# The keys' maximum one projection group later, and the first weights on ScalarE's DMA queue, in a fused attention and Fourier-filter kernel

## The chip, the core and the metric

The kernel runs on one core of one Trainium2 chip. The metric is the device time of one execution in microseconds (us); lower is better. The core has TensorE (PE, matrix products), VectorE (DVE), ScalarE (ACT), GpSimd (POOL) and SyncE (SP), each with its own instruction queue that it works through in order, and 16 DMA engines that SP, ACT and POOL give transfers to.

## The reference

Two independent results are computed from two inputs of 2048 tokens by 448 channels and put side by side.

```python
q = (x @ wq).reshape(B, S, H, Dh)          # H = 16 heads, Dh = 28
k, v = x @ wk, x @ wv                      # one key and one value head for all 16
p = softmax(q k^T * Dh**-0.5)
a = concat_heads(p @ v) @ wo               # first half of the output
X = rfft2(x_b, axes=(tokens, channels)) * (w_r + 1j * w_i)
b = irfft2(X)                              # second half of the output
```

## The kernel before

The kernel has two stages. The **first stage**, up to about 70 us, projects the tokens to queries, keys and values and does the first half of the Fourier transform. The **second stage**, the remaining 560 us, is attention with the rest of the transform woven in; its order of work on TensorE, VectorE and ScalarE is written out by hand (`PLAN`). The change touches only the first stage, which ends where the first score product (L918) starts.

Single precision is carried by splitting every operand into a rounded high part and a remainder: `split_x` and `split_w` copy a raw tile to the high part and subtract to get the low part, and `proj` multiplies high by high, high by low and low by high. Tokens are worked in four chunks `c` of 512, projected outputs in four groups `g` of 128, channels in four parts `j`. Chunk 0 and the first part of chunk 1 are done part by part while their data arrive; after that the loop `for c ... for g` does one group at a time: eight or eleven projection products, `evac(c, g)` (ScalarE copies the result to `qraw`, VectorE reduces it to the largest absolute value, `qmx`), and behind some groups a unit of the transform.

A unit `q` of the transform (there are eight) has a load, a fold, a first product `fft1_a` (64 small matmuls, L155) and a second product `fft1_b` (16 matmuls, L174). The fold runs on VectorE: two operations on the halves (L130), a sum and a difference (L132, L133), which `fft1_fold(q, 0)` issues, and four more (L136 to L139), which `fft1_fold(q, 1)` issues; without a part it issues all eight.

The softmax is shifted by a bound instead of a true maximum. For this the largest absolute key is needed once: `qm` (L459, VectorE) reduces `qmx` of the first two groups over all chunks, `key_max` (L377 to L380) brings it into place with two matmuls (four passes) on TensorE and copies it to `kmb` on VectorE, `terms` (L286, VectorE) multiplies `kmb` with the queries' maxima, and `shift` (L291, L292) sums on TensorE and copies to `cvec` on VectorE. It is done for chunk 0 first, so that `build_q(0, 0)` (L232, L234, L223) can make the first query tile, and for the other chunks at the end (`terms(1, NC)`, `shift(1, NC)`, then `cmax`, L483, which the small products L487 check against a limit). The keys are also collected: `fetch` moves rows of `qraw` to `kf`, on SP or on POOL's DMA queue, and 16 transposes (L498) turn the values.

The order on TensorE in the first stage is the order of the program. The order on the other engines is made by a scheduler from dependences and priorities; `behind(a, b)` adds that `a` is issued after `b` on its engine, without a wait between engines. Raw tiles (256 KB each) come from a pool named `raw` with eight buffers, the weights' first tile in three pieces, and all of these transfers are issued by SP.

Of the kernel before, what the change touches and what calls it, by code (L numbers as in the profile page):

```python
# [10 lines left out]
F32 = mybir.dt.float32  # L11
# [4 lines left out]
ALU = mybir.AluOpType  # L16
# [49 lines left out]


WARM = 10, 6


@with_exitstack
def kernel(ctx: ExitStack, tc: tile.TileContext, t: dict):
    nc = tc.nc
# [49 lines left out]
    def fft1_fold(q, part=None):  # L123
        x = xb[q][0][:113]
        e2, o2 = x[:, 0:2], x[:, 2:4]
        if part != 1:
            f = ff[q] = fp.tile([113, 4, 4, 2, 32], F32, name="f", tag="wi")
            xv = x.rearrange("p k (j h m) -> p k j h m", h=2, m=32)
            for h, op in enumerate((ALU.add, ALU.subtract)):
                nc.vector.tensor_tensor(f[:, :, :, h], xv[:, :, :, 0], xv[:, :, :, 1], op=op)  # L130
            y = f.rearrange("p k j h m -> p k (j h m)")
            nc.vector.tensor_tensor(e2, y[:, 0::2], y[:, 1::2], op=ALU.add)  # L132
            nc.vector.tensor_tensor(o2, y[:, 0::2], y[:, 1::2], op=ALU.subtract)  # L133
        if part != 0:
            y = ff[q].rearrange("p k j h m -> p k (j h m)")
            return [nc.vector.tensor_tensor(y[:, 0], e2[:, 0], e2[:, 1], op=ALU.add),  # L136
                    nc.vector.tensor_tensor(y[:, 1], e2[:, 0], e2[:, 1], op=ALU.subtract),
                    nc.vector.tensor_tensor(y[:, 2], o2[:, 0], o2[:, 1], op=ALU.subtract),
                    nc.vector.tensor_tensor(y[:, 3], o2[:, 0], o2[:, 1], op=ALU.add)]  # L139

    at1, stored = {}, []

    def fft1_a(q):
        for p in range(2):
# [112 lines left out]
    with tc.tile_pool(name="w1", bufs=1) as w1:  # L257
# [27 lines left out]
        def terms(c0, c1):  # L285
            return nc.vector.tensor_scalar(prod[:, :, c0:c1], qmx[:, :, c0:c1], kmb, None, op0=ALU.mult)  # L286
# [6 lines left out]

        halves = slice(0, 1024), slice(1024, 2048)
        with tc.tile_pool(name="x1", bufs=2) as x1:
            warm = x1.tile([1, 1], F32, name="warm")
            nc.vector.memset(warm, 0.0)
            nc.scalar.activation(warm, warm, AF.Exp)
# [9 lines left out]
                zeros(n)  # L308

            def raw(src, eng):  # L310
                r = x1.tile([128, 512], F32, name="raw", bufs=8)
                eng.dma_start(r, src)
                return r


            first = slice(0, 128), slice(128, 256), slice(256, 512)
            xr, wr = {}, {}
            xr[0, 0] = raw(t["xa"][0, :, 0], nc.sync)
            wr[0] = x1.tile([128, 512], F32, name="raw", bufs=8)
            for s in first:  # L320
                nc.sync.dma_start(wr[0][:, s], t["wq"][:, 0, s])

            xr[1, 0] = raw(t["xa"][1, :, 0], nc.sync)
            for j in range(1, NK):
                xr[0, j] = raw(t["xa"][0, :, j], nc.sync)
                wr[j] = x1.tile([128, 512], F32, name="raw", bufs=8)
                for s in (slice(0, 256), slice(256, 512)):
                    nc.sync.dma_start(wr[j][:, s], t["wq"][:, j, s])

# [23 lines left out]
            def proj(pq, xh, xl, g, j, some=(0, 1, 2)):  # L353

                gs = slice(g * 128, (g + 1) * 128)
                parts = ((wqh, xh), (wqh, xl), (wql, xh)) if j < 3 else ((wqh, xh), (wql, xh))
                for n, (w, x) in enumerate(parts):
                    if n in some:
                        mm(pq, w[:, j, gs], x[:, j], start=(j == 0 and n == 0), stop=(j == 3 and n == 1))

            def evac(c, g, pq):
                cs = slice(c * CW, (c + 1) * CW)
                out = nc.scalar.activation(qraw[:, g, cs], pq, AF.Copy)
                nc.vector.tensor_reduce(qmx[:, g, c:c + 1], qraw[:, g, cs], axis=AX.X, op=ALU.max,
                                        apply_absolute_value=True)
                return out
# [8 lines left out]
            def key_max():  # L375

                pb = bank()  # L377
                for k in range(2):
                    mm(pb[:, 0:1], sel[:, k], qm[:, k:k + 1], start=(k == 0), stop=(k == 1))
                nc.vector.tensor_copy(kmb, pb[:, 0:1])  # L380
# [42 lines left out]
            for c in range(1, NC):  # L423
                for g in range(NG):
                    pq = pq1[g] if c == 1 else bank()
                    for j in range(1 if c == 1 else 0, NK):
                        proj(pq, *xs[c], g, j)
                    last = evac(c, g, pq)
                    if g == 0 and c < 3:
                        parts_of(c + 1)  # L430
                        for j in range(NK):
                            split_x(*xs[c + 1], c + 1, j)
                            if c < 2:
                                xr[c + 2, j] = raw(t["xa"][c + 2, :, j], nc.sync)
                    if c == 1 and g == 1:
                        fetch(range(7), halves[0])
                    if c == 3 and g == 1:
                        fetch(range(7), halves[1])
                    if c == 2 and g == 3:
                        fetch(range(7, 14), slice(0, 1536), nc.gpsimd)  # L440
                    if c == 3 and g == 2:
                        fetch(range(7, 12), slice(1536, S), nc.gpsimd)
                    if c == 1 and g == 0:
                        fft1_fold(1)
                    if c == 2 and g == 3:
                        keys(0)
                    n = 4 * (c - 1) + g
                    if n in slots:
                        q = slots.index(n)
                        fft1_a(q)  # L450
                        fft1_load(q + 4)
                        if n == 10:

                            terms(0, 1)
                            shift(0, 1)
                            qf, qh, ql = build_q(0, 0, True)
                        if n == 9:

                            top = nc.vector.tensor_reduce(qm, qmx[:, 0:2], axis=AX.X, op=ALU.max)  # L459
                            for ins in fft1_fold(5, 1):  # L460
                                behind(ins, top)
                        if q < 6:
                            fft1_fold(q + 2, None if q not in (3, 5) else 0)
                        if q:
                            fft1_b(q - 1)
                        if n == 9:
                            key_max()
            fetch(range(12, 14), slice(1536, S), nc.gpsimd)


# [5 lines left out]
            copy_q(i, 3, qf, ql, nc.gpsimd)  # L476
        behind(copy_q(1, 1, qf, ql, nc.scalar), last)
        top = terms(1, NC)
        for ins in fft1_fold(7, 1):
            behind(ins, top)  # L480
        last = fft1_b(5)
# [26 lines left out]
    d, f, a, b, e, c = free  # L508
# [450 lines left out]
    c = NC - 1  # L959
# [227 lines left out]
```

## Time and profile before

| what | us |
|---|---|
| median of three runs | 635.23 (634.75 to 635.24) |
| the profiled execution's own time | 635.08 |
| its span in the profile | 633.3 |
| busy in the span: PE | 627.4 (99%) |
| busy: DVE | 439.9 (69%) |
| busy: ACT | 546.9 (86%) |
| granted TensorE clock | 1.0 throughout |

All times in the profile are microseconds from the span's start; a row of the timeline gives start, duration, engine, line, operation and tiles, and in brackets the engine's idle time before it with what ended it. PE is the matmul row, PEld the loading of weights beside it. Matmuls overlap, so what one costs is read from start to start.

### The profile page before, as it was taken

The page shows a single profiled execution, that of the slowest core. Times are in us where ns is not written, and L with a number is a line of the kernel's source. Part 1 is how long each engine was busy: PE and PEld are TensorE (multiplying, and loading weights), DVE is VectorE, ACT ScalarE, POOL GpSimd, SP SyncE. Part 2 cuts the span into 40 slices and gives each one's busy share as a digit, 9 for nine tenths or more (in the row PEclk, how much of TensorE's full clock was granted, in tenths as well). Part 3 has the DMA queues.
Part 4 walks back from the last instruction along what each step waited for, and adds up shares of the span by engine and source line. Part 5 has one row for each costly group of instructions (what it writes and reads, how often), then busy time and mean ns, then how long its engine had stood idle before and what let it go on. Part 6 is the DMA issues. An engine that isn't in the chain of part 4 may idle for free. (4 is left out here: it accounts for less than half of the span.)

```text
span 633.3 us, 12165 instructions
## 1 busy us (share of the span) xinstructions
PE 627.4 (99%) x4437; PEld 377.7 (60%) x4437; DVE 439.9 (69%) x793; ACT 546.9 (86%) x984; POOL 61.5 (10%) x118
## 2 busy tenths in 40 slices
PE   9999999999999999999999999999999999999997
PEld 7877645646565655646565665565566565555555
DVE  5999648789998943866766845277687764457653
ACT  5554999999999998988989989998989989989991
POOL 4021501011113110000110100001010100000000
PEclk9999999999999999999999999999999999999999
DMA  8865863456455522216340513034152413030011
GB/s 254 288 177 168 261 167 87 115 146 177 124 152 124 139 65 66 76 64 187 77 106 18 125 37 82 16 83 147 35 129 60 98 55 91 16 82 11 21 31 61
DMA packets 37891, 66.74 MB, mean 105 GB/s; under 512 B 8009, under 2 KB 22746, under 8 KB 36860
## 3 DMA queue, kind: packets, MB, share of 16 engines
q1 hardware_dynamic: 32608, 52.50, 30.2%
q0 software_dynamic: 4640, 12.48, 7.7%
q8 instruction: 36, 0.59, 0.4%
q10 hardware_dynamic: 576, 0.92, 0.4%
q14 instruction: 31, 0.25, 0.1%
HBM read 29.81 MB, written 17.87 MB: 75 GB/s over the span
## 5 line engine op out<-in xcount | busy, mean ns | idle before, releaser
L853 ACT ACTIVATE p<-s 128x512 f32<-128x512 f32 x405 | 222.1, 638 | 27.3 <-PE s L918 26.5
L918 PE MATMUL s<-qa,ka 128*128 128x512 f32 x756 | 227.6, 402 | 0.0
L918 PEld LDWEIGHTS s<-qa,ka 128*128 128x128 f32 x756 | 138.1, 188 | 60.9 <-issue 26.8
L924 DVE COPY k<-s 128x512 f32<-128x512 f32 x122 | 80.1, 684 | 62.9 <-PE s L918 62.7
L864 PE MATMUL s<-p,vs 128*32 128x512 f32 x976 | 121.3, 595 | 0.0
L853 ACT ACTIVATE qraw<-s 128x512 f32<-128x512 f32 x137 | 79.2, 655 | 6.5 <-PE s L918 6.5
L943 ACT ACTIVATE k<-k 128x1024 f32<-128x1024 f32 x80 | 83.5, 1145 | 0.0
L864 PEld LDWEIGHTS s<-p,vs 128*32 128x32 f32 x976 | 29.4, 109 | 64.3 <-issue 59.4
L918 PE MATMUL sx<-qa,ka 128*128 128x512 f32 x137 | 55.3, 403 | 0.0
L918 PE MATMUL po<-qa,ka 128*128 128x512 f32 x131 | 53.2, 406 | 0.0
L853 ACT ACTIVATE p<-po 128x512 f32<-128x512 f32 x75 | 48.2, 642 | 4.5 <-PE po L918 4.2
L864 PE MATMUL s<-qraw,vs 128*32 128x512 f32 x384 | 49.5, 593 | 0.0
L853 ACT ACTIVATE p<-sx 128x512 f32<-128x512 f32 x64 | 41.5, 649 | 3.0 <-PE sx L918 2.9
L738 POOL DMA_DIRECT2D ol<-ol x36 | 18.0, 508 | 229.0 <-DVE ol L761 156.9
L864 PE MATMUL s<-k,vs 128*32 128x512 f32 x304 | 39.7, 594 | 0.0
L918 PEld LDWEIGHTS sx<-qa,ka 128*128 128x128 f32 x137 | 25.7, 188 | 11.1 <-issue 4.2
L918 PEld LDWEIGHTS po<-qa,ka 128*128 128x128 f32 x131 | 24.6, 188 | 11.3 <-issue 5.0
L868 DVE STREAM_TRANSPOSE osb<-s 128x512 f32<-128x512 f32 x13 | 9.3, 716 | 28.0 <-PE s L864 27.9
L864 PEld LDWEIGHTS s<-qraw,vs 128*32 128x32 f32 x384 | 12.0, 110 | 27.3 <-issue 26.1
L924 DVE COPY k<-po 128x512 f32<-128x512 f32 x17 | 11.6, 685 | 21.4 <-PE po L918 21.3
L853 ACT ACTIVATE qraw<-sx 128x512 f32<-128x512 f32 x35 | 22.9, 653 | 2.0 <-PE sx L918 2.0
L924 DVE COPY p<-s 128x512 f32<-128x512 f32 x35 | 23.0, 681 | 0.0
(277 smaller groups left out, 973.5 us busy)
## 6 DMA issues: line engine op xcount, KB each, us to landing
qa<-qa SPq DMA_DIRECT2D x15, 512.0 KB
raw<-xa SPq DMA_DIRECT2D x16, 256.0 KB
xb<-xb SPq DMA_DIRECT2D x8, 512.0 KB
qa<-qh SPq DMA_DIRECT2D x64, 64.0 KB
qa<-ql SPq DMA_DIRECT2D x60, 64.0 KB
t<-bs SPq DMA_DIRECT2D x16, 225.0 KB
wr<-wr POOLq DMA_DIRECT2D x16, 225.0 KB, 3.8
wi<-wi POOLq DMA_DIRECT2D x16, 225.0 KB, 5.2
```

Of the source, the lines that this page charges most:

```text
L738: nc.gpsimd.dma_start(ol[c][o, g].bitcast(F32), ol[c][r, 0].bitcast(F32))
L853: nc.scalar.activation(tiles[-1][:, h % 2], sc, AF.Exp, scale=SCALE)
L864: mm(po[c, g][32 * i:32 * i + 32], vs[:, kc], ps[i // 2][:, i % 2], start=(n == 1), stop=(n == 16))
L868: nc.vector.transpose(o, po[c, g])
L918: begun.append(mm(sc, ka[:, kc * 128:(kc + 1) * 128], qa[c, g][:, h], start=True, stop=True))
L924: nc.vector.tensor_copy(keep[i][h // 2][:, h % 2], sc)
L943: nc.scalar.activation(p, p, AF.Exp, scale=SCALE)
```

## The change

Two edits go together.

- The keys' maximum: `key_max()` moves from the end of the transform's unit behind group (3, 1) to directly behind the projection products of group (3, 2), ahead of that group's evacuation. The fold of unit 6 is cut in two parts like those of 5 and 7, and its last four operations are issued behind `terms(0, 1)`. For units 6 and 7 the last operation of the first part (L133 before) is issued behind `terms(0, 1)` and `terms(1, NC)`.
- The start: the three pieces of the first weights' tile are issued by ScalarE, ahead of its first activation, instead of by SP between the first two token tiles. The pool `raw` has twelve buffers instead of eight.

```diff
+RAW = 12
...
-            nc.vector.tensor_tensor(o2, y[:, 0::2], y[:, 1::2], op=ALU.subtract)
+            fold_end[q] = nc.vector.tensor_tensor(o2, y[:, 0::2], y[:, 1::2], op=ALU.subtract)
...
+            first = slice(0, 128), slice(128, 256), slice(256, 512)
+            xr, wr = {}, {}
+            wr[0] = x1.tile([128, 512], F32, name="raw", bufs=RAW)
+            for s in first:
+                nc.scalar.dma_start(wr[0][:, s], t["wq"][:, 0, s])
             warm = x1.tile([1, 1], F32, name="warm")
             nc.vector.memset(warm, 0.0)
             nc.scalar.activation(warm, warm, AF.Exp)
...
             xr[0, 0] = raw(t["xa"][0, :, 0], nc.sync)
-            wr[0] = x1.tile([128, 512], F32, name="raw", bufs=8)
-            for s in first:
-                nc.sync.dma_start(wr[0][:, s], t["wq"][:, 0, s])
 
             xr[1, 0] = raw(t["xa"][1, :, 0], nc.sync)
...
                     for j in range(1 if c == 1 else 0, NK):
                         proj(pq, *xs[c], g, j)
+                    if (c, g) == (3, 2):
+                        key_max()
                     last = evac(c, g, pq)
...
-                            terms(0, 1)
+                            top = terms(0, 1)
+                            behind(fold_end[6], top)
+                            for ins in fft1_fold(6, 1):
+                                behind(ins, top)
                             shift(0, 1)
...
-                            fft1_fold(q + 2, None if q not in (3, 5) else 0)
+                            fft1_fold(q + 2, None if q < 3 else 0)
                         if q:
                             fft1_b(q - 1)
-                        if n == 9:
-                            key_max()
...
         top = terms(1, NC)
+        behind(fold_end[7], top)
         for ins in fft1_fold(7, 1):
             behind(ins, top)
```

More of the change, by code (lines that the diff above doesn't have):

```diff
@@ L310, in raw @@
             def raw(src, eng):
-                r = x1.tile([128, 512], F32, name="raw", bufs=8)
+                r = x1.tile([128, 512], F32, name="raw", bufs=RAW)
                 eng.dma_start(r, src)
                 return r
-            first = slice(0, 128), slice(128, 256), slice(256, 512)
-            xr, wr = {}, {}
             xr[0, 0] = raw(t["xa"][0, :, 0], nc.sync)
-            wr[0] = x1.tile([128, 512], F32, name="raw", bufs=8)
-            for s in first:
-                nc.sync.dma_start(wr[0][:, s], t["wq"][:, 0, s])
             xr[1, 0] = raw(t["xa"][1, :, 0], nc.sync)
@@ L325 @@
                 xr[0, j] = raw(t["xa"][0, :, j], nc.sync)
-                wr[j] = x1.tile([128, 512], F32, name="raw", bufs=8)
+                wr[j] = x1.tile([128, 512], F32, name="raw", bufs=RAW)
                 for s in (slice(0, 256), slice(256, 512)):
```

2 lines of the change are left out of this document (1 added, 1 removed).

## The prediction

> **What bounds the kernel now.** I read the page's engine parts first, then the stretches of ten microseconds of the first stage, then the timeline of each engine around the places that the change touches, and last what waits for the keys' collected rows.
>
> ```profile
> PE 627.4 (99%) x4437; PEld 377.7 (60%) x4437; DVE 439.9 (69%) x793; ACT 546.9 (86%) x984; POOL 61.5 (10%) x118
> 40.00:50.00 10.00, 10.00 (x115) 7.88 (x112) 9.96 (x20) 5.18 (x9) 1.38 (x3) 1.00 0.59 164
> 50.00:60.00 10.00, 9.27 (x180) 6.97 (x178) 9.93 (x25) 4.36 (x8) 2.33 (x5) 1.00 0.65 185
> 60.00:70.00 10.00, 10.00 (x203) 7.89 (x200) 9.23 (x23) 7.18 (x13) 5.54 (x11) 1.00 0.76 206
> PE s L379 <- DVE qm L459: 0.7, 1, 0.7
> ```
>
> The columns of the stretches are PE, PEld, DVE, ACT and POOL busy, granted clock, DMA share, GB/s. TensorE is busy 99% of the span, so the time is the sum of its matmuls and its few gaps. In the first 72 us its own list of waits has, apart from the wait for the very first instruction, one entry: the 0.7 us of the keys' maximum, which is the 9.27 of 50 to 60. VectorE is busy 9.96 and 9.93 of 10 there: it is the second bound, a few tenths behind. In attention TensorE's gaps come to nothing that the list shows, so whatever shifts the first score product at 69.64 shifts the end by as much. A change of the first stage is therefore worth what it takes from TensorE's chain up to 69.64, and no more than VectorE and the transfers let through.
>
> **The change part by part. The old place of the maximum.** TensorE's timeline, a normal hand-over from the transform to a projection group first, then the one with the maximum, then the hand-over where the maximum will stand:
>
> ```profile
> 39.73 0.36 PE L174 MATMUL po<-a,fw 64*64 64x225 f32 x2
> 40.01 0.50 PE L359 MATMUL s<-xh,wqh 128*128 128x512 f32 x1
> 52.91 0.36 PE L174 MATMUL po<-a,fw 64*64 64x225 f32 x2
> 53.99 0.61 PE L379 MATMUL s<-qm,sel 128*128 128x1 f32 x4 [0.73 <-DVE qm L459]
> 54.46 0.49 PE L359 MATMUL s<-xh,wqh 128*128 128x512 f32 x1
> 56.87 0.39 PE L359 MATMUL s<-xh,wql 128*128 128x512 f32 x1
> 57.19 1.76 PE L155 MATMUL s<-cs,f 113*32 113x113 f32 x64
> ```
>
> From start to start the normal hand-over is 40.01 - 39.73 = 0.28 us, the one with the maximum 54.46 - 52.91 = 1.55. Taking it out saves 1.27 us.
>
> **The new place.** The four passes do not vanish; they now stand between the last projection product of group (3, 2) and the transform's 64. What such an insertion costs is shown by `shift`, two passes between the transform's products, against the same stretch without it:
>
> ```profile
> 32.06 1.76 PE L155 MATMUL s<-cs,f 113*32 113x113 f32 x64
> 33.74 0.41 PE L174 MATMUL pbb<-a,fw 64*64 64x225 f32 x2
> 58.88 0.39 PE L291 MATMUL s<-prod,blk 128*128 128x4 f32 x2
> 59.19 0.41 PE L174 MATMUL pbb<-a,fw 64*64 64x225 f32 x2
> ```
>
> Without: 33.74 - 32.06 = 1.68. With: 59.19 - 57.19 = 2.00. So two passes cost 0.32, which is the lower end; the upper end is the 0.61 that the four passes were busy. I take 0.45, near the 0.47 from 53.99 to 54.46. Net of this part: -1.27 + 0.45 = **-0.82 us**, between -0.95 and -0.66, if the maximum finds its input ready and nobody waits for its output. Both are read from VectorE:
>
> ```profile
> 53.06 0.68 DVE L364 TENSOR_REDUCE qmx<-qraw 128x1 f32<-128x512 f32 x1
> 53.78 0.16 DVE L459 TENSOR_REDUCE qm<-qmx 128x2 f32<-128x8 f32 x1
> 55.20 1.28 DVE L130 TENSOR_TENSOR f<-xb 113x512 f32<-113x512 f32 x2
> 56.40 0.15 DVE L380 COPY kmb<-s 128x1 f32<-128x1 f32 x1
> 57.73 0.22 DVE L286 TENSOR_SCALAR prod<-qmx,kmb 128x4 f32<-128x4 f32 x1
> 63.06 0.68 DVE L133 TENSOR_TENSOR xb<-f 113x512 f32<-113x512 f32 x1
> 64.38 0.23 DVE L286 TENSOR_SCALAR prod<-qmx,kmb 128x12 f32<-128x12 f32 x1
> ```
>
> `qm` is ready at 53.94. In the changed kernel TensorE comes to the maximum at about 56.87 - 1.27 + 0.3 = 55.9, so that wait is gone with two microseconds to spare. The copy to `kmb` can then run at about 56.4, where VectorE already has it now. `terms(0, 1)` follows; what waits for it is `shift(0, 1)` on TensorE, at 58.88 - 0.82 = 58.1. Before, it ended at 57.95, 0.15 ahead of that; the new ties put it ahead of the last fold operation L133, 0.6 us earlier, so it has cover of 0.75. The four later operations of unit 6 stay behind it as they are now, and their reader `fft1_a(6)` is 4 us away. I cost the ties of unit 6 at nothing. The tie of unit 7 does the same for `terms(1, NC)`: it took place at 64.38, behind L133 at 63.06, and TensorE will ask for it at 65.44 - 0.82 = 64.6 (row below); moved ahead of L133 it is ready by about 64.0. Without the tie it would be a stall of up to 0.1.
>
> **The start.** Issues and first consumers, and two of the stretches of one microsecond (columns as above):
>
> ```profile
> 0.76 0.41 SPq L312 DMA_DIRECT2D raw<-xa  x1
> 1.23 1.36 SPq L321 DMA_DIRECT2D raw<-wq  x3
> 3.95 0.43 DVE L345 CAST xh<-raw 128x512 fp32r<-128x512 f32 x1 [2.90 <-DMA raw<-xa]
> 4.15 0.51 ACT L339 ACTIVATE wqh<-raw 128x128 fp32r<-128x128 f32 x2 [1.89 <-DMA raw<-wq]
> 4.52 0.72 PE L359 MATMUL s<-xh,wqh 128*128 128x512 f32 x1
> 2.00:3.00 1.00, 1.00 (x6) 0.70 (x5) 0.00 (x0) 0.24 (x2) 0.94 (x2) 1.00 0.92 272
> 3.00:4.00 1.00, 1.00 (x6) 0.75 (x5) 0.05 (x1) 0.00 (x0) 1.00 (x3) 1.00 0.79 200
> 17.43 1.29 DVE L130 TENSOR_TENSOR f<-xb 113x512 f32<-113x512 f32 x2 [0.98 <-DMA xb<-xb]
> ```
>
> The first product starts 0.14 us after the first token tile is cast (3.95 + 0.43 = 4.38) and about as long after the first weights' piece is copied (half of 0.51 behind 4.15, 4.40). Both have to come earlier for the start to move, and the token tile was already issued first, at 0.76. The change issues the weights' pieces at the same moment from another queue. So the weights may come up to 0.47 us earlier (1.23 - 0.76), which alone is worth nothing, and the token tile may come later by what is mixed into it: one piece is 64 KB, at the 272 GB/s of the stretch 2 to 3 that is 0.24 us; all 256 KB would be 0.96. The other end is a gain: the first weights' piece took 4.15 - 1.23 = 2.92 from issue to use and the token tile 3.19; if the tile came as quickly, 0.27. I take **+0.1 us**, between the gain and one piece, nearer to the piece, because all that is certain is that the two now share the engines from the first byte.
>
> The Trainium skill (DMA: Bandwidth & Descriptors, "Issuing engines are not separate DMA queues") says that transfers started by ScalarE and SP run on the same 16 DMA engines and interleave, and that starting them from several engines saves only the issuing time. It speaks against this edit for the first token tile and leaves the queue behind it its issuing time; by it alone the start would be 0.24 later instead of 0.1, and the sum 0.14 less of a gain. No row of the kernel before has two such queues at work at once.
>
> What the edit does give is SP's time: 1.36 us of issuing lie between the first and the second token tile, and the DMA engines had room meanwhile (200 GB/s where they had moved 272, a share of 0.79). The next tiles come earlier by 72 KB at 272 GB/s, 0.26 us, up to 1.36. TensorE does not wait for them (its list has no such wait). VectorE does: it sat idle for 0.98 us before 17.43, waiting for the first unit's tile, and is full from there on. So VectorE's whole chain can start earlier by 0 to 0.98; I take **0.3**. ScalarE's three issues, at some 0.45 each, hold its first activation back until about 2.1 and with its table load to about 3.5; it is needed at 4.15, so this costs nothing, and has 0.6 of cover. The four added buffers let SP run ahead; the engines already work off a backlog when it first waits for a buffer, so beyond the 0.3 I give that nothing.
>
> **What is late next.** With TensorE 0.72 earlier (0.82 less 0.1), two things that had slack come into view:
>
> ```profile
> 66.07 0.17 DVE L483 TENSOR_REDUCE cmax<-cvec 128x4 f32<-128x16 f32 x1
> 65.44 0.39 PE L291 MATMUL s<-prod,blk 128*128 128x12 f32 x2
> 66.68 0.32 PE L487 MATMUL s<-sel,cmax 128*1 128x4 f32 x7
> 68.53 1.17 PE L498 MATMUL s<-ident,kf 32*128 32x32 f32 x16
> 69.64 2.24 PE L918 MATMUL s<-qa,ka 128*128 128x512 f32 x8
> 63.43 1.03 POOL L211 DMA_DIRECT2D qa<-ql  x2 [3.27 <-DVE ql L223]
> 64.45 1.02 POOL L273 DMA_DIRECT2D kf<-qraw  x2
> DMA to landing us min/median/max: 4.2/4.2/4.2
> kf<-qraw POOLq DMA_DIRECT2D x7, 8.0 KB, 2.8
> ```
>
> First, `cmax` ended at 66.24 and its reader started at 66.68: a lead of 0.44. VectorE's work ahead of `cmax` is the same, only in another order, so `cmax` comes earlier only by VectorE's 0.3. TensorE needs it at 66.68 - 0.72 = 65.96 and gets it at 65.94. That holds by a hair; without the 0.3 it would cost 0.28.
>
> Second, the last two rows of keys and values that POOL fetches (issued from 64.45, the second at 64.97) landed 4.2 us after issue (the answer for `kf` from 63 to 70 us), so at 69.2. The transposes run from 68.53 to 69.64, and the last four of the 16, which read those tokens, start at about 69.36: a lead of 0.2. The fetch stands in POOL's queue behind two copies of the query tile, which wait for VectorE's `ql`, so it too moves only with VectorE, to 68.9, where TensorE now wants it at 68.64: a stall of 0.25. But 4.2 is slow for this transfer; the median of its seven is 2.8, and with that it is 1.1 early. So 0 to 0.55 (without VectorE's 0.3); I take **+0.15**.
>
> **The sum.** -0.82 + 0.1 + 0.15 = -0.57 us. Against the profiled execution, 635.08, that is 634.5; the median of the three runs, 635.23, lies 0.15 above it, so by the runs 634.7. I say **634.6 us**, 0.1% faster than the median. A measurement of this kernel can tell about 0.2%, 1.27 us, from no change (its runs themselves span 0.5 us), so this forecast counts as no difference.
>
> **The rivals.** *Everything is kept and the start gains too.* The maximum costs only the 0.32 of two passes (-0.95), the fetch takes 2.8, and the first token tile takes that time too instead of 3.19: ready at 3.56 instead of 3.95, 0.39 earlier, with the weights' piece copied at about 3.94 just in time for it. That is -1.34, so 633.7 from the profiled 635.08 and 633.9 from the median, at the edge of what counts as faster. For it: the fetch's median, and that VectorE may gain up to 0.98. Against it: two queues share one set of engines.
>
> *The wait only moves.* VectorE is no earlier, `cmax` is 0.28 late, and behind it the fetch takes 4.2 again, so that TensorE reaches the scores at most 0.2 earlier (the fetch's lead); with a piece of the weights in front of the tile (0.24) nothing is left: 635.2. For it: 9.93 to 9.96 of 10 on VectorE. Against it: the 0.98 us that VectorE waited for a transfer.
>
> *Slower: VectorE is made to wait for the maximum.* Its order is fixed beforehand. If the copy to `kmb` is put directly behind `qm` in its queue, VectorE stands from 53.94 until TensorE has done the maximum, about 56.4: 2.5 us in which the whole queue behind it (the rest of folds 5, 6 and 7, the query tile, `cvec`, `cmax`) stands too. Taking off VectorE's 0.3 and the lead of 0.44, TensorE would lose 1.8 us at L487: about 637.0. It decides from 2.0 us of standing (0.3 + 0.44 + 1.27). Put behind fold 5's last four, the standing is 1.2 us and the loss 0.4, 635.6. For it: VectorE now takes the copy 1.8 us after TensorE had it ready, so that the order is not one of readiness. Against it: in the old order the first two operations of the next fold (55.20 to 56.4) already stand ahead of the copy.
>
> *The change does not do what it says* can only be the start, if the pieces from ScalarE land no earlier; that is inside the forecast.
>
> **How the numbers follow.** Forecast (net loss of TensorE's wait, part of it paid back): 0.52. Everything kept: 0.25, of which I count 0.22 beyond 0.2%, the rest inside. The wait only moves: 0.11, inside. Slower: 0.12, of which 0.1 beyond 0.2%. So faster 0.22, same 0.68, slower 0.1. The range goes from 633.8, the second case between its two readings, to 635.6, the mild end of the slower case; what is left out is its severe end (0.1) and a start still earlier than the second case has it, under 0.2 together.
>
> **What the changed profile would show.** TensorE: no wait before L379 on `qm`, and L379 between L359 and L155 with some 0.45 us from start to start beyond the 0.32 of an ordinary hand-over; the score product L918 near 69.1. VectorE: L130 of the first unit near 17.1, `terms` ahead of L133, `cmax` near 65.9. Start: the cast L345 at 3.9 to 4.2; if it is later than 4.4, the start is mis-sized. I am wrong in sign if VectorE shows a gap of more than a microsecond before L380, or L918 starts after 69.64; I am wrong in size if TensorE waits at L487 or in L498.

## The result and the profile after

The changed kernel is slower. Its median is 635.58 us (22 runs, 635.27 to 639.54) beside 634.99 us for the kernel before (22 runs on the same chip); the ratio is **1.0014, 95% interval 1.0009 to 1.0020**. That is 0.6 to 1.3 us, on the other side of zero from the forecast. The span of its profiled execution is 634.0 us, before 633.3.

First the page of the changed kernel, two stretches of its first stage (PE, PEld, DVE, ACT, POOL busy, granted clock, DMA share, GB/s), and TensorE's own list of waits up to 72 us:

```profile
PE 627.4 (99%) x4437; PEld 377.7 (60%) x4437; DVE 440.2 (69%) x793; ACT 547.0 (86%) x984; POOL 61.4 (10%) x118
50.00:60.00 10.00, 10.00 (x178) 8.04 (x181) 8.21 (x20) 4.65 (x9) 2.19 (x5) 1.00 0.63 176
60.00:70.00 10.00, 9.83 (x209) 7.47 (x202) 9.78 (x26) 7.30 (x14) 4.33 (x9) 1.00 0.65 170
PE s L311 <- DVE idle L307: 1.1, 1, 1.1
PE s L360 <- ACT wqh L340: 0.9, 2, 0.5
PE s L492 <- DVE cmax L488: 0.2, 1, 0.2
```

TensorE does the same 627.4 us of work. The 0.7 us wait for `qm` is gone, and two others are there in its place: 0.9 us at the very start for the copied weights `wqh` (L340 is L339 before), and 0.2 us for `cmax`. VectorE, which was full from 50 to 60, now has almost two microseconds of idle time there.

TensorE's timeline at the places of the change. The first and the last row are the first transform product and the first score product; before, they started at 25.14 and 69.64:

```profile
26.54 0.69 PE L156 MATMUL s<-cs,f 113*32 113x113 f32 x20
57.01 0.39 PE L360 MATMUL s<-xh,wql 128*128 128x512 f32 x1
57.24 0.50 PE L380 MATMUL s<-qm,sel 128*128 128x1 f32 x4
57.67 1.76 PE L156 MATMUL s<-cs,f 113*32 113x113 f32 x64
65.92 0.39 PE L292 MATMUL s<-prod,blk 128*128 128x12 f32 x2
67.41 0.32 PE L492 MATMUL s<-sel,cmax 128*1 128x4 f32 x7 [0.17 <-DVE cmax L488]
69.25 1.18 PE L503 MATMUL s<-ident,kf 32*128 32x32 f32 x16
70.36 0.50 PE L923 MATMUL s<-qa,ka 128*128 128x512 f32 x1
```

From the first transform product to the first score product it takes 70.36 - 26.54 = 43.82 us, before 69.64 - 25.14 = 44.50. So in this pair of executions the middle gained 0.68 us. But the first transform product is 1.40 us later, and the sum, +0.72, is what the span shows (634.0 - 633.3). The loss happened in the first microseconds:

```profile
0.76 1.39 ACTq L301 DMA_DIRECT2D raw<-wq  x3
4.48 0.43 DVE L346 CAST xh<-raw 128x512 fp32r<-128x512 f32 x1 [3.43 <-DMA raw<-xa]
4.64 0.31 ACT L340 ACTIVATE wqh<-raw 128x128 fp32r<-128x128 f32 x1 [0.96 <-DMA raw<-wq]
5.06 0.47 PE L360 MATMUL s<-xh,wqh 128*128 128x512 f32 x1 [0.35 <-ACT wqh L340]
5.86 0.31 ACT L340 ACTIVATE wqh<-raw 128x128 fp32r<-128x128 f32 x1 [0.91 <-DMA raw<-wq]
7.02 0.42 ACT L340 ACTIVATE wqh<-raw 128x256 fp32r<-128x256 f32 x1 [0.85 <-DMA raw<-wq]
7.49 0.50 PE L360 MATMUL s<-xh,wqh 128*128 128x512 f32 x1 [0.53 <-ACT wqh L340]
16.13 1.29 DVE L131 TENSOR_TENSOR f<-xb 113x512 f32<-113x512 f32 x2 [0.67 <-DMA xb<-xb]
```

The third piece in the kernel before:

```profile
5.30 0.42 ACT L339 ACTIVATE wqh<-raw 128x256 fp32r<-128x256 f32 x1 [0.65 <-DMA raw<-wq]
```

The three pieces of the first weights' tile are issued about half a microsecond earlier than before, and the third is copied 7.02 - 5.30 = 1.72 us later. TensorE stands for it. The first token tile (L346) is 0.53 later too. Of the 1.40 us, 0.54 is there at the first product (5.06, before 4.52) and 1.30 at the first product of the third piece (7.49, before 6.19); the last 0.1 is that this product and the next start 0.34 apart instead of 0.23. The first unit's tile, on the other hand, lets VectorE start 17.43 - 16.13 = 1.3 us earlier.

### The profile page after: what moved, and what is told of

Read it like the earlier page. It is cut to its first block, busy times and chain, and to the rows that moved or that the text cites. A ratio compares the mean times of both kernels' runs of the same rounds, so it can differ in the third digit from the quotient of the medians.

```text
span 634.0 us, 12161 instructions
## 1 busy us (share of the span) xinstructions
PE 627.4 (99%) x4437; PEld 377.7 (60%) x4437; DVE 440.2 (69%) x793; ACT 547.0 (86%) x984; POOL 61.4 (10%) x118
## 5 line engine op out<-in xcount | busy, mean ns | idle before, releaser
L360 PE MATMUL s<-xh,wqh 128*128 128x512 f32 x56 | 22.8, 407 | 0.9 <-ACT wqh L340 0.9
```

## The experiments

Each ratio is to the kernel before on the same chip, with a 95% interval; 0.001 is 0.63 us. "Third piece" is the start of its copy and "middle" the time from the first transform product to the first score product, both in the profiled execution.

| run | median us | ratio | third piece | middle |
|---|---|---|---|---|
| before | 634.99 | 1 | 5.30 | 44.50 |
| changed | 635.58 | 1.0014 (1.0009 to 1.0020) | 7.02 | 43.82 |
| start alone | 635.75 | 1.0018 (1.0007 to 1.0029) | 6.96 | 43.76 |
| maximum alone | 634.90 | 0.9999 (0.9990 to 1.0008) | 6.65 | 43.82 |
| buffers alone | 634.76 | 0.9998 (0.9989 to 1.0007) | 5.03 | 44.01 |
| maximum and buffers | 634.81 | 1.0002 (0.9993 to 1.0011) | 5.02 | 43.83 |
| maximum without ties | 634.98 | 1.0005 (0.9996 to 1.0014) | 5.66 | 44.92 |
| quiet SP | 634.72 | 1.0002 (0.9993 to 1.0011) | 5.29 | 43.82 |
| late check | 634.65 | 0.9999 (0.9990 to 1.0008) | 5.78 | 43.62 |

The profiled execution is one of many: that of maximum alone was the slowest of its runs (635.92 us beside the median of 634.90), and its third piece, on SP's queue, came at 6.65. A late piece is thus possible with one queue, too; with SP issuing, the others came at 5.0 to 5.8. Verdicts rest on the ratios. The start scatters, too: the first transform product came at 25.14 to 26.16 us in the eight profiles with SP issuing the weights, and at 25.81 to 26.54 in the four with three strided pieces on ScalarE's queue, so that the pair shown above, 25.14 and 26.54, holds the two ends. And the second stage is not a fixed stretch: from the first score product to the end of the span it takes 563.1 to 564.4 us in the twenty profiles, with a wait of TensorE for `oh` near 367 us of up to 0.81 in it. Some tenths won or lost in the first stage of a profile need not show in its total.

**The parts alone.** The first theory was that the start edit holds the loss; its rival, that the moved maximum does (VectorE's order, or the wait for `cmax`). *Start alone* is the kernel before with the start edit and twelve buffers:

```diff
+            wr[0] = x1.tile([128, 512], F32, name="raw", bufs=RAW)
+            for s in first:
+                nc.scalar.dma_start(wr[0][:, s], t["wq"][:, 0, s])
...
-            for s in first:
-                nc.sync.dma_start(wr[0][:, s], t["wq"][:, 0, s])
```

> The start edit alone (ScalarE's queue for the first weights' pieces, twelve raw buffers) on the kernel before. Theory A, the start costs and the maximum gains: the pieces share the DMA engines packet by packet with SP's token tiles; the third piece is copied at about 7.0 us instead of 5.3, TensorE's stream is 1.4 us later by 25 us, and the whole is 1.0 to 1.4 us slower than before (about 636.2). Theory B, the moved maximum with its ties on VectorE costs the time: the start is hidden and this kernel is within 0.3 us of before.

It has all of the loss, 1.0018. *Maximum alone* is the changed kernel with these lines put back and `RAW = 8`:

> The moved maximum with its ties alone, start and buffers as before. Theory A: TensorE's wait of 1.27 us is gone against some 0.45 us of new cost, so 0.5 to 0.8 us faster than before (about 634.3); the first score product near 69.0 us. Theory B: VectorE's wait for the maximum (0.9 us in the changed kernel) is paid at cmax, so no faster than before, up to 0.9 us slower.

0.9999: the moved maximum neither gains nor loses anything that can be measured; the -0.82 us of the prediction, a ratio of 0.9987, lies outside its interval. *Buffers alone* is the kernel before with `bufs=12`, and *maximum and buffers* the changed kernel with SP issuing the weights as before:

> Twelve raw buffers alone. Theory A: within 0.3 us of before, first score product at 69.6 plus or minus 0.2. Theory C, SP running ahead through the free buffers crowds the engines: slower by some 0.5 us or more, with the first weights' pieces as early as before and a later token or weights' tile waited for by TensorE.

> The moved maximum with its ties and twelve buffers, all first transfers by SP as before: the changed kernel without ScalarE's queue. Theory A: the start is that of the kernel before, 1.0 us earlier than the changed kernel's; the stretch from the first transform unit to the first score product 43.8 us (44.0 with the old maximum and twelve buffers), so 0.1 to 0.4 us faster than before, 634.5.

Neither differs from the kernel before. So the loss needs the weights on ScalarE's queue.

**Why the moved maximum gains nothing.** Three other profiles have the maximum in its old place: buffers alone, start alone, and a kernel described at the end (before, with rows moved). None has a wait for `qm`. For two of them, the first unit's first fold operation and the end of VectorE's way to the maximum, then the maximum on TensorE. Buffers alone:

```profile
16.99 1.29 DVE L131 TENSOR_TENSOR f<-xb 113x512 f32<-113x512 f32 x2 [0.64 <-DMA xb<-xb]
53.28 0.16 DVE L460 TENSOR_REDUCE qm<-qmx 128x2 f32<-128x8 f32 x1
53.60 0.61 PE L380 MATMUL s<-qm,sel 128*128 128x1 f32 x4
```

Before, with rows moved, and the hand-over around the maximum:

```profile
16.49 1.29 DVE L130 TENSOR_TENSOR f<-xb 113x512 f32<-113x512 f32 x2 [0.72 <-DMA xb<-xb]
52.75 0.16 DVE L459 TENSOR_REDUCE qm<-qmx 128x2 f32<-128x8 f32 x1
53.15 0.36 PE L174 MATMUL po<-a,fw 64*64 64x225 f32 x2
53.44 0.61 PE L379 MATMUL s<-qm,sel 128*128 128x1 f32 x4
53.90 0.48 PE L359 MATMUL s<-xh,wqh 128*128 128x512 f32 x1
```

In the first profile of the kernel before, the fold started at 17.43 and `qm` at 53.78. In these three (before, buffers alone, rows moved), the later the first unit's tile lands, the later is `qm`: 17.43, 16.99, 16.49 give 53.78, 53.28, 52.75. (In start alone VectorE stood 0.36 us for `qraw` on the way, and 16.28 gives 53.37.) TensorE came by at 53.26 where it had to wait (53.99 - 0.73), and at 53.60, 53.44 and, in start alone, 54.52. So the wait of 0.73 us on which the prediction was built is an outcome of one execution, in which the first unit's tile came latest and TensorE earliest of the four. In the others the old place costs no wait: the hand-over takes 53.90 - 53.15 = 0.75 us, not 1.55. The middle then takes 43.66 us (25.38 to 69.04, rows moved) and 43.76 (start alone), no longer than the 43.82 of the moved maximum; the 44.01 of buffers alone has in it a wait of 0.20 for the fetched rows `kf`.

**The ties.** *Maximum without ties* is maximum alone without the `behind` calls, with unit 6's fold in one piece again:

```diff
-                            top = terms(0, 1)
-                            behind(fold_end[6], top)
-                            for ins in fft1_fold(6, 1):
-                                behind(ins, top)
+                            terms(0, 1)
...
-        behind(fold_end[7], top)
```

> The moved maximum without its ties on VectorE (fold of unit 6 whole again), start and buffers as before. Theory A, TensorE's gain runs into VectorE's chain at cmax whatever the ties: the stretch from the first transform unit to the first score product is 43.8 us as with the ties, plus at most 0.2 for terms behind L133. Theory B, the ties make VectorE stand (0.5 us in the kernel with the moved maximum alone) and so cost: without them the stretch is 43.5 or less and cmax's reader does not wait.

```profile
58.59 0.42 DVE L140 TENSOR_TENSOR f<-xb 113x256 f32<-113x256 f32 x1
58.93 0.15 DVE L381 COPY kmb<-s 128x1 f32<-128x1 f32 x1
59.11 0.23 DVE L287 TENSOR_SCALAR prod<-qmx,kmb 128x4 f32<-128x4 f32 x1
59.45 0.36 PE L292 MATMUL s<-prod,blk 128*128 128x4 f32 x2 [1.30 <-ACT a L162]
67.23 0.32 PE L488 MATMUL s<-sel,cmax 128*1 128x4 f32 x7
```

VectorE does all of unit 6's fold first, and TensorE stands 1.30 us in `shift(0, 1)`. The row names ScalarE's copy `a`, but the operand that came last is `prod`, which ends at 59.34. In the profile the middle is 1.1 us longer than with the ties (44.92 beside 43.82), more than either theory had; in the runs the ratio is 0.0006, 0.4 us, above that of maximum alone, and the intervals overlap. The last row belongs to the other tie, that of unit 7: without it the check products do not wait for `cmax`, and come 67.23 - 65.98 = 1.25 us behind `shift(1, NC)`, where with the ties they come 1.49 behind.

**The wait for `cmax`.** *Late check* is maximum and buffers with the check products behind the first half of unit 7's product, and the query copies behind `cmax` alone:

```diff
+        fft1_a_out(7, 0, fft1_a_mm(7, 0))
...
-            behind(copy_q(i, 0, qf, qh, nc.vector), top if i < 2 else bound)
+            behind(copy_q(i, 0, qf, qh, nc.vector), top)
...
-        fft1_a_out(7, 0, fft1_a_mm(7, 0))
```

> As the kernel with the moved maximum and twelve buffers, and in addition the small products that read cmax stand behind the first half of unit 7's first product, with the four query copies behind cmax alone. Theory A, what is left of the gain is held back by cmax: TensorE's wait of 0.2 us there goes, the stretch from the first transform unit to the first score product is 43.5 to 43.6 us, and the whole is 0.3 to 0.6 us faster than before. Otherwise a new wait shows at the score products for the query copies, or at unit 7's first product for its fold, and the stretch stays 43.8.

TensorE's wait goes and the middle shortens by 0.21 us, to 43.62. The 0.3 to 0.6 us that were expected of the total did not come: 0.9999, with an interval that cannot show so little as 0.21.

**Why a second queue costs time.** The first theory: SP, freed of the pieces, runs ahead with large rows while ScalarE's pieces come in small rows, and the DMA engines serve the two queues in turn. *Quiet SP* is the changed kernel with three tiny loads (`mask`, `sgn`, `sel4`), which SP issues later in the changed kernel, moved behind the first token tile:

```diff
             xr[0, 0] = raw(t["xa"][0, :, 0], nc.sync)
+            mask = const("mask", [128, 1], nc.sync)
+            sgn = const("sgn", [128, 1], nc.sync)
+            sel4 = const("sel4", [128, 4], nc.sync)
```

> The changed kernel with three tiny constant loads (0.5 to 2 KB each) put into SP's queue where the weights' pieces stood, so that SP's second token tile is issued as late as before while the pieces go by ScalarE. Theory A: with only one token tile to share with, the third piece is copied by about 5.0 to 5.5 us, TensorE's stream at 25 us is at most 0.4 us later than before and the whole is 0.8 to 1.2 us faster than the changed kernel (634.4 to 634.8). Theory D, ScalarE's queue itself is late (its three issues ahead of the table load, or a slower queue): the third piece is copied at about 7 us again and the time is that of the changed kernel, 635.6.

The loss goes (1.0002), with the weights still on ScalarE's queue; the third piece comes as before the change:

```profile
5.29 0.42 ACT L343 ACTIVATE wqh<-raw 128x256 fp32r<-128x256 f32 x1 [0.59 <-DMA raw<-wq]
```

So it is SP's running ahead beside the pieces that costs, and not ScalarE's issuing. How the queues share is seen in the DMA view of the changed kernel from 2 to 5 us (q1 is SP's, q10 ScalarE's; packets, MB, share of 16 engines):

```profile
q1 hardware_dynamic: 326, 0.60, 64.2%
q10 hardware_dynamic: 298, 0.15, 22.6%
```

Nearly packet for packet: 326 to 298. But a row of a piece is 512 bytes or 1 KB and a row of SP's tiles 2 KB, so ScalarE's queue moves a fifth of the bytes. The Trainium skill (DMA: Bandwidth & Descriptors, "Queues, rings and completion order") says that each DMA engine goes round the queues it has work for, one packet from each; a packet there holds some 9 to 17 descriptors, so it need not be what this view counts. The equal counts agree with such turns. Quiet SP, from 3 to 4 us, shows the same turns with the sizes the other way round, for there SP's queue is sending its tiny loads:

```profile
q10 hardware_dynamic: 177, 0.10, 32.4%
q1 hardware_dynamic: 164, 0.04, 22.2%
```

The counts are again nearly equal, and now ScalarE's queue moves more than twice SP's bytes.

By that theory, pieces with larger rows should do better. *One transfer* is the changed kernel with the first weights' tile in a single transfer of 2 KB rows:

```diff
-            for s in first:
-                nc.scalar.dma_start(wr[0][:, s], t["wq"][:, 0, s])
+            nc.scalar.dma_start(wr[0], t["wq"][:, 0])
```

> The changed kernel with the first weights' tile as one transfer of 2 KB rows on ScalarE's queue instead of three pieces of 0.5 and 1 KB rows; SP's queue as in the changed kernel, free to run ahead. Theory A, the two queues take turns packet by packet, so that small packets get a small share of the bytes: with 128 packets of 2 KB against 128 of the token tile, the whole weights' tile is there by about 4.5 us, TensorE does not wait for a weights' copy beyond 0.4 us, the first transform unit (L155 before) starts by about 25.6 instead of 26.5, and the whole is 0.6 to 1.0 us faster than the changed kernel. Theory D, what counts is only how many bytes are ahead in all queues: SP's second and third tile are there as before, the weights' tile lands at about 6.5 to 7 us, and the time is no better than the changed kernel's 635.6.

637.70 us, ratio 1.0051 (1.0037 to 1.0065, five runs), was the worst of all. In its profile, of a run of 638.95 us, both first tiles came about two microseconds later than in the changed kernel, and fewer packets of SP's were served in 2 to 5 us:

```profile
6.33 0.82 ACT L339 ACTIVATE wqh<-raw 128x128 fp32r<-128x128 f32 x3 [3.64 <-DMA raw<-wq]
6.51 0.43 DVE L345 CAST xh<-raw 128x512 fp32r<-128x512 f32 x1 [5.46 <-DMA raw<-xa]
8.81 0.63 PE L359 MATMUL s<-xh,wqh 128*128 128x512 f32 x1
q1 hardware_dynamic: 207, 0.39, 50.8%
q10 hardware_dynamic: 112, 0.21, 34.5%
```

The late tiles are not the whole loss. TensorE waits 2.38 us for them, and its first product is 2.56 us later than in the kernel before; from 8.38 us on, ten products then take 0.63 us each (the third row is one), 0.43 from start to start, where before they took 0.39 and 0.23. By the first transform product (30.01) the delay has grown to 4.87. The granted clock is 1.00 all through, and no row shows why the products were slow.

So turns alone did not explain it. *Quiet SP with one transfer* joins the two edits:

> The first weights' tile as one transfer on ScalarE's queue, with SP's next token tile held back by three tiny loads. The one-transfer kernel without them took 637.7 us, half of the engines landing both first tiles 1.5 to 2 us late. Theory E, what delays the first tiles is SP's queue running ahead beside them: with it held back the first product starts before 5.2 us instead of 7.1 and the whole is back at 634.5 to 635.2. Theory F, two queues reading 2 KB rows at once are slow in themselves: the first product still starts after 6 us, 636.5 or more.

1.0022 (1.0013 to 1.0032), with five runs at 634.9 to 635.1 and six at 636.4 to 637.2: something now costs 2 us in some executions and nothing in others. Each theory had one half of this; the profile, of a run of 634.93, does not show the other.

The second theory was placement: the token tile `xa[0, :, 0]` and the weights' part `wq[:, 0]` are both read in 2 KB rows out of an 8 KB stride, from the same offset. Three kernels lay each part down in one piece in memory, so that its rows follow each other (`.transpose(2, 0, 1, 3)` for `xa`, no transpose for `wq`); the transfers stay, with other addresses. One transfer, contiguous:

> The one-transfer kernel with the token and weights' tiles each contiguous in memory (256 KB runs instead of 2 KB rows 8 KB apart), same transfers otherwise. Theory G, the rows 8 KB apart of the first tiles fall on the same part of the memory and slow one another when two queues read them: contiguous, the first product starts by 5.2 us and the time falls from 637.7 to 635 or less. Theory E, order and amount alone count: no change, 637 to 638.

The changed kernel, contiguous:

> The changed kernel with contiguous token and weights' tiles. Theory A, turns by packet: the third weights' piece is copied at 6.5 us or later again, the time stays at 635.3 to 635.8. Theory G, memory: the piece is copied by 5.5 us, the time falls to 634.5.

Late check, contiguous (SP issues all):

> The kernel with the moved maximum, twelve buffers, SP's start and the late check of cmax, with contiguous tiles. If memory rows slow the start of every version, the first transform unit starts at 24.9 instead of 25.4 and the whole is 0.3 to 0.8 us faster than before; otherwise it equals the same kernel with the old layout, 634.65, within 0.3.

They gave 634.95 us, ratio 1.0012 (1.0002 to 1.0022, three of its twelve runs still at 636.8 to 637.2); 634.94, 1.0003 (0.9994 to 1.0012); and 634.87, 1.0000 (0.9991 to 1.0009). Contiguous rows take away most of the loss where two queues read, and do nothing where one does. The changed kernel and its contiguous form once more, on one chip:

> The changed kernel itself, on the same chip as the next one: 1.0009 to 1.002 of before, the first transform unit at 26.3 or later in the profile.

> The changed kernel with contiguous tiles, beside the changed kernel. Theory G, memory: 0.5 us or more below the changed kernel's median, no wait of TensorE for a weights' copy. Theory A, turns by packet alone: the same time as the changed kernel within 0.3 us.

635.29, ratio 1.0017 (1.0008 to 1.0026), and 634.78, 1.0002 (0.9993 to 1.0010): both repeated, 0.51 us apart. The theory of turns had put down no difference here. To tell the offset from the stride, *one transfer, rows moved* keeps the stride and puts the weights' parts two places further round:

```diff
-            nc.scalar.dma_start(wr[0], t["wq"][:, 0])
+            nc.scalar.dma_start(wr[0], t["wq"][:, 2])
...
-                    nc.sync.dma_start(wr[j][:, s], t["wq"][:, j, s])
+                    nc.sync.dma_start(wr[j][:, s], t["wq"][:, (j + 2) % NK, s])
...
-    z["wq"] = wq.reshape(D, 512)[rows].reshape(NK, 128, 512).transpose(1, 0, 2)
+    z["wq"] = np.roll(wq.reshape(D, 512)[rows].reshape(NK, 128, 512), 2, 0).transpose(1, 0, 2)
```

> The one-transfer kernel (637.7 us) with the weights' four parts stored in another order in memory, so that the first part's rows lie 4 KB further in their 8 KB stride than the first token tile's offset pattern had them; rows stay 2 KB, 8 KB apart. Theory G1, the two first tiles fall on the same part of the memory: moved, they do not, and the time falls to 635 or less. Theory G2, rows 8 KB apart are slow to read from two queues wherever they lie: 637 to 638 again.

634.31 us, 0.9995 (0.9987 to 1.0004), from 637.70 with nothing changed but the place:

```profile
3.80 0.82 ACT L339 ACTIVATE wqh<-raw 128x128 fp32r<-128x128 f32 x3 [1.11 <-DMA raw<-wq]
3.99 0.51 DVE L345 CAST xh<-raw 128x512 fp32r<-128x512 f32 x1 [2.94 <-DMA raw<-xa]
```

That looked like the answer for the changed kernel too. It is not. The changed kernel and the kernel before with the same move, and one transfer, rows moved, with the late check:

> The changed kernel with one thing altered: the parts of the weight tiles lie two places further round in memory, so that the first weights' part no longer lies at the offset, within its 8 KB stride, of the first token tile. The instructions are the same. Theory of placement (two queues that read rows at the same offset of an 8 KB stride at the same time hold each other up): the changed kernel's 0.6 to 0.8 us over the kernel before goes, ratio 0.9990 to 1.0004, and TensorE's first transform unit starts before 26.2. Theory of turns (the small packets of ScalarE's queue lose to SP's larger ones wherever they lie): it stays at a ratio of 1.0010 to 1.0025.

> The kernel before with the same two places of turn in memory and nothing else. There one queue reads token tile and weights' part one after the other. Placement between two queues: nothing, ratio 0.9995 to 1.0005. If the place as such costs (whichever queue reads it): a gain of 0.4 us or more, ratio 0.9993 or less.

> What the runs point to, together: the changed kernel with each weights' part in one transfer, the parts two places further round in memory, and the check products of the maximum behind the first half of unit 7's product. Placement: 0.2 to 0.3 us under the same kernel without the late check products (which gave 0.9995), so a ratio of 0.9985 to 0.9995. Theory of turns: no better than 1.0000.

The changed kernel keeps its whole loss, 635.59 us, 1.0014 (1.0005 to 1.0023); the kernel before is unmoved, 634.78, 1.0001 (0.9992 to 1.0010); and the joined kernel gives 634.78, 1.0003 (0.9994 to 1.0012), where placement had foreseen 0.9985 to 0.9995. In the changed kernel with rows moved, the third piece is late again, though the first token tile (3.57) and the first piece are early:

```profile
3.55 0.29 ACT L340 ACTIVATE wqh<-raw 128x128 fp32r<-128x128 f32 x1
6.30 0.42 ACT L340 ACTIVATE wqh<-raw 128x256 fp32r<-128x256 f32 x1 [1.74 <-DMA raw<-wq]
```

With the rows at the old place, one transfer costs 1.0051 and three 1.0014; with them moved, one costs 0.9995 and three still 1.0014. So placement within the stride is what spoiled the single transfer, and it is not what the changed kernel loses, as far as one other place can tell. That loss goes when SP is held back, which is what the theory of turns says. But it goes with contiguous rows too, which turns alone do not explain. Equal turns are seen with the loss and without it: in 2 to 5 us the two queues had 386 and 391 packets in one contiguous profile and 420 and 394 in the other. What differs is how many there were: 777 and 814 together, beside 624 in the changed kernel and 587 to 713 in the four strided profiles. The third piece came at 6.32 and 5.93 there, beside 7.02, 6.96, 6.47 and 6.30 in the strided ones. So the turns were shorter with contiguous rows; that this is the whole repair is not shown.

Nor does the single transfer at the good place show that large rows cure the changed kernel. In its profile the first score product starts at 69.90, no earlier than the 69.64 of the changed kernel with rows moved; the lower time of that execution (634.79 beside 635.47) arises behind it. **Open** are why rows at one offset of the stride cost two queues so much, why the turns are shorter with contiguous rows, and how the changed kernel's loss divides between the turns and the layout. None of these kernels is faster than the kernel before by more than its interval; the lowest is 0.9995 (0.9987 to 1.0004).

## Why the prediction was wrong

**The start is the term that was mis-sized, and it turned the sign of the sum.** It was put at +0.1 us. It is +1.40 in the profile, at the first transform product (between the two ends of its scatter), and a ratio of 1.0018 alone, 0.4 to 1.8 us. The working looked at the first token tile and the first piece of the weights. There 0.54 us was lost in this profile, beyond its range of -0.27 to +0.24, though within the 0.96 that it named for the whole tile; in the changed kernel with rows moved nothing was (the first product at 4.35). What it left out is the last piece, the rest of the 1.40. In the kernel before, all three stood ahead of SP's next tiles in one queue; in a queue of their own they share every turn with those tiles, and the third was 1.72 late. The prediction took the tiles that SP sends earlier as a gain for VectorE, and did not ask what they are sent ahead of. The rule that it quoted from the Trainium skill (DMA: Bandwidth & Descriptors, "Issuing engines are not separate DMA queues"), that such transfers interleave and only issuing time is saved, pointed the right way; the 0.24 worked out from one piece was too small, because the whole tile is delayed. Two marks that the prediction set were passed: a cast later than 4.4 for a mis-sized start (4.48), a first score product after 69.64 for a wrong sign (70.36).

**The time itself, 635.58, lies 0.02 inside the upper end of the stated range, and that is luck.** The upper end was the mild case of a rival that did not happen, and the range stood on 635.08 to 635.23; the kernel before was at 634.99 beside the changed one, and 1.0014 of 635.08 would be 636.0.

**The old place was sized from one execution.** The -1.27 us is right for the profile that it was read from. Of it 0.73 was the wait, which the three other profiles of the old order don't have. There the hand-over takes 0.75 to 0.76 us, 0.28 of which is ordinary, so that the removal is worth 0.47 to 0.48; 0.34 for the new place and 0.25 for `cmax` take that back: +0.11 to +0.12, about what 43.82 against 43.66 and 43.76 shows. So -0.82 became nothing (0.9999).

**The new place** costs less than was predicted: from the last projection product to the transform it takes 57.67 - 57.01 = 0.66 us, 0.32 of which is the ordinary hand-over (57.19 - 56.87), so 0.34, predicted 0.45 and at least 0.32. In the changed profile -1.27 + 0.34 + 0.25 = -0.68 is all that the middle gained.

**VectorE 0.3 us earlier** was 1.3, more than its bound of 0.98. Here, too, 17.43 is the late end of a scatter: the fold's first operation started at 16.48 to 17.43 in the eight profiles with SP issuing the weights, and at 15.69 to 16.28 in the four with three strided pieces on ScalarE's queue. VectorE gave it back in waits for work that hangs on TensorE: 0.75 for `qraw` and 0.91 for `kmb`. VectorE's timeline of the changed kernel:

```profile
52.72 0.69 DVE L365 TENSOR_REDUCE qmx<-qraw 128x1 f32<-128x512 f32 x1 [0.75 <-ACT qraw L364]
57.78 0.16 DVE L381 COPY kmb<-s 128x1 f32<-128x1 f32 x1 [0.91 <-PE s L380]
57.97 0.23 DVE L287 TENSOR_SCALAR prod<-qmx,kmb 128x4 f32<-128x4 f32 x1
58.11 0.68 DVE L134 TENSOR_TENSOR xb<-f 113x512 f32<-113x512 f32 x1
64.78 0.23 DVE L287 TENSOR_SCALAR prod<-qmx,kmb 128x12 f32<-128x12 f32 x1
64.92 0.69 DVE L134 TENSOR_TENSOR xb<-f 113x512 f32<-113x512 f32 x1
67.18 0.17 DVE L488 TENSOR_REDUCE cmax<-cvec 128x4 f32<-128x16 f32 x1
```

**`cmax` "by a hair"** did not hold: 0.17 us of wait. From `shift(1, NC)` to the check products it takes 67.41 - 65.92 = 1.49, before 66.68 - 65.44 = 1.24, a loss of 0.25. The prediction said that VectorE's work ahead of `cmax` is the same, only in another order. The order is what costs: the tie of unit 7 has put L134 between `terms(1, NC)` and `cmax`, so that from `prod` to `cmax` it takes 67.18 - 64.78 = 2.40, before 66.07 - 64.38 = 1.69. It is not that VectorE stood for `kmb`. In quiet SP it does not, and TensorE waits the same 0.17:

```profile
56.93 0.15 DVE L384 COPY kmb<-s 128x1 f32<-128x1 f32 x1
66.46 0.32 PE L492 MATMUL s<-sel,cmax 128*1 128x4 f32 x7 [0.17 <-DVE cmax L488]
```

**The ties.** `terms` stands ahead of the fold's last operation at both places (57.97 and 64.78). That of unit 6 was right: without it TensorE stood 1.30 us. That of unit 7 was not: it was to save up to 0.1, and costs the 0.25 at `cmax`. It was to have `terms(1, NC)` ready 0.6 earlier, but `terms` reads the `qmx` reduced just before it; behind the transform's product it comes 64.78 - 63.32 = 1.46, before 64.38 - 62.83 = 1.55, only 0.09 earlier. **The fetch** was put at +0.15 and cost nothing: from transposes to scores it takes 70.36 - 69.25 = 1.11, before 69.64 - 68.53 = 1.11; in buffers alone, TensorE did wait 0.20 for its rows. **The buffers** were right at nothing (0.9998). The rival that came out slower, VectorE made to wait for the maximum, is seen at 57.78, but the 0.91 of idle time there cost TensorE nothing that the profiles show; the slower case that happened, in the transfers, had no rival, and so no chance of its own. That a shift of the first score product shifts the end by as much holds only to some tenths, as the 563.1 to 564.4 us behind it show.

## What to carry to other kernels

Giving a second DMA queue the first-needed data takes away its place in the line: ask what the first queue now sends at the same time, with what row size, and when the *last* piece that the compute engine needs has landed. A wait between two engines that run nearly level is a property of an execution; look for it in a second profile before taking its length as the gain. An operation that is held back on a full engine delays what now stands behind it: follow the new order to its next reader. Two edits in one change are tested apart first: here one was all of the loss and the other nothing.

## What was not expected of the hardware

- Two queues that read 2 KB rows at the same offset of an 8 KB stride: 637.70 us (1.0051); with the weights' rows moved by 4 KB within the stride: 634.31 (0.9995), with the same transfers. Where one queue reads both, the same move does nothing (1.0001).
- From 2 to 5 us, two queues share by packets and not by bytes: 326 to 298 packets, 0.60 to 0.15 MB. With SP's queue on tiny loads, from 3 to 4 us: 164 to 177 packets, 0.04 to 0.10 MB.
- Three tiny loads behind the first tile, which keep SP's queue busy with small rows, took the whole loss away (1.0002, 0.9993 to 1.0011).
- After a wait of 2.38 us in the one-transfer kernel, ten products of TensorE took 0.63 us each instead of 0.39, while the granted clock stood at 1.00.
